# The opening of a delta-rule attention and feed-forward kernel: loads of values and queries moved, identity products added, beta's load moved forward

## The chip, the cores and the metric

The kernel runs on one core of a Trainium2 chip. A core has five engines that run their own instruction streams in order and meet at semaphores: PE (TensorE, matrix products and transposes into PSUM; its weight loads are listed as PEld), DVE (VectorE), ACT (ScalarE), POOL (GpSimd) and SP (SyncE, which here only issues DMA transfers). The metric is the time of one execution in microseconds (us). Before the change the median of three runs is 647.78 us (647.63 to 649.5). One further execution was profiled; the trace comes from that one.

## The reference

Two blocks follow each other. The first is a delta-rule recurrence over 768 positions, for 4 batches and 8 heads of 48 dimensions:

```python
k_n = k / (np.linalg.norm(k, axis=-1, keepdims=True) + 1e-06)
state = np.zeros((B, H, D, D))
for t in range(S):
    kt, vt, bt = (k_n[:, :, t], v[:, :, t], beta[:, :, t, None])
    y[:, :, t] = np.einsum('bhd,bhde->bhe', q[:, :, t], state)
    v_old = np.einsum('bhde,bhd->bhe', state, kt)
    state = state + bt[:, :, :, None] * np.einsum('bhd,bhe->bhde', kt, vt - v_old)
```

Its output, as 3072 tokens of 384 numbers, goes through a feed-forward block with a slope for negative values:

```python
h = x @ w_in                     # 384 -> 2048
g = np.maximum(h, 0.0) + alpha * np.minimum(h, 0.0)
return g @ w_out                 # 2048 -> 384
```

All of it is in 32-bit floats.

## The kernel before

The 768 positions are cut into 12 chunks of 64. A step is one chunk of two of the four batches, so there are 24 steps, numbered in order; steps 0 and 1 are the first chunk, 2 and 3 the second. Within a step the recurrence is solved in closed form: the Gram matrix of the keys is made on PE (`grams`, L486), a triangular inverse of it on DVE, and products on PE with it give the corrected values, the output and the new state. Two finished steps make 256 tokens, which go through the feed-forward block on PE (`ffn_in` L1075, `ffn_out` L1118 and faster forms later). From about 43 us on, this feed-forward work is woven between the attention pieces of later steps, so that PE always has something to do. Before that there is none, and the kernel is a chain of small pieces: this is the opening, and the change lies in it and in the function behind it.

All the order is written out by hand (the block `manual_schedule`): every engine executes its instructions in the order in which the program text makes them. What the reader needs of it:

- Loads. `load_early(n)` loads the key of step n (two transfers of 96 KB), into one of four tiles `ke0` to `ke2` and `kl1`. The first three keys are issued half on SP and half on ACT; everything else is issued by SP, one after the other. `load_v` and `load_q` load values and queries, two transfers per step. `beta_sb` (L188) is one transfer of 96 KB. `fetch_in(n)` issues the loads of the first n pieces of `w_in`, each 512 KB, into staging space; there are twelve pieces, p0 to p11 here, and `w_out` comes in sixteen pieces after them, by the same function.
- Weight conversion. Each staged piece is worked on by ACT twice (L240 and L242, `begin_in`), by DVE once (L256) and by POOL once (L263). Only then may PE use it. The feed-forward product of chunk 0 takes p0, p1, p2 for its first 12 products, p3, p4, p5 for the next 12, and so on, one piece for each third of the contraction.
- `pause(n, upto)` is a one-element write by POOL (L1668) into a staging tile that is still in use; the loads that `fetch_in(upto)` issues into that tile have to wait for it. So the point in POOL's order at which the write stands sets when the load may start.
- The opening, steps 0 to 3 together: PE makes the five `identities` (L1551) while the first loads come, then transposes of the keys (`flipped`, L430), Gram matrices (L486), transposes of beta (`betas`, L330), transposes of the queries (`query_flip`) and `queries` (L1567). ACT squares the keys (`squared`, L386), copies transposes out of PSUM and scales (`pick`, `raw`). DVE sums (`norms`, L393), picks the diagonal blocks (L643), and then runs `eliminate_small`, a triangular inverse in 28 dependent instructions. `signs` are four small instructions, alternating between DVE (L338) and ACT (L340), that take beta out of PSUM.
- While DVE eliminates, PE transposes keys 4 to 6 and queries 2 and 3 and fills the rest with products that nobody reads: `busy(n, p)` (L1539) multiplies n times 512 columns of the tile `ke2` with the identity.
- `first_chunk` then does steps 0 and 1: `place_small` (L706, DVE), `scale_first` (L845, values times norms), `matrix` and `own_values` (L857), three rounds (L857 on PE, L912 on DVE), `outputs`, `to_ffn`.
- `second_pair` does steps 2 and 3 with the feed-forward products of chunk 0 between (`alongside(products, pieces)` puts so many products of `ffn_in` and so many half steps of weight conversion there). POOL scales the values of steps 2 and 3 here (`scale_first`), and makes the turned copies `turn_matrix` and `turn_values` (L873).

Of the kernel before, what the change touches and what calls it, by code (L numbers as in the profile page):

```python
# [39 lines left out]
STAGED = 4  # L40
# [3 lines left out]
def kernel(  # L44
# [11 lines left out]
    nc = tc.nc  # L56
# [17 lines left out]
    doubles, big, ffn_banks = ExitStack(), [], []  # L74
# [49 lines left out]
    ident = const.tile([128, 128], FP32, name="ident")  # L124
# [14 lines left out]
    def load_early(n, *queues):  # L139
        if n < N:  # L140
            fetch(k, n, early(n)[:, :, 0:D], *queues)
# [15 lines left out]
    def load_q(n):  # L157
        if n < N:
            fetch(q, n, q_pad[n % NQ][:, :, 0:D])

    def load_v(n):
        if n < N:
            v_raw[n] = work.tile([128, H, D], FP32, name="v_raw", bufs=3)
            fetch(v, n, v_raw[n])
# [14 lines left out]
        mybir.EngineType.PE, mybir.EngineType.DVE, mybir.EngineType.Activation,  # L179
        mybir.EngineType.Pool, mybir.EngineType.SP,  # L180
    }))
    for i in range(2):
        load_early(i, (nc.sync, nc.scalar))

    SPACES = 3
    space_out = const.tile([128, SPACES, DM * 2], U32, name="space_out")
    beta_sb = space_out.rearrange("p s e -> p (s e)")[: B * H, 0:S].bitcast(FP32)
    nc.sync.dma_start(out=beta_sb, in_=beta.rearrange("b h s -> (b h) s"))  # L188
    load_early(2, (nc.scalar, nc.sync))

    w_in = const.tile([128, KT, DFF], FP32, name="w_in")
# [133 lines left out]
    def betas(first, last, p):  # L325
        n = last - first
        p = p[:, 0 : n * B * H].rearrange("p (c b t h) -> p c b t h", c=n, b=NB, t=2)
        for c in range(n):
            at = (first + c) * 128
            nc.tensor.transpose(  # L330
                p[:, c].rearrange("p b t h -> p (b t h)"), beta_sb[:, at : at + 128],
                ident[: B * H, : B * H],
            )
        to = beta_t.rearrange("p (c i) b h -> p i c b h", i=2)[:, :, first:last]

        def turned_sign(t, i):
            if i == 0 and first == 0:
                nc.vector.tensor_scalar_mul(to[half(t), i], p[half(i), :, :, t], -1.0)  # L338
            else:
                nc.scalar.mul(to[half(t), i], p[half(i), :, :, t], -1.0)  # L340

        return [lambda t=t, i=i: turned_sign(t, i) for t in range(2) for i in range(2)]
# [41 lines left out]
    def squared(n):  # L384
        ksq[n] = work.tile([128, H, D], FP32, name="ksq", bufs=2)
        nc.scalar.square(ksq[n], early(n)[:, :, 0:D])  # L386
# [13 lines left out]
    def weigh(n):  # L400
        if n >= N:
            return []
        norm = stats[n]
        root(norm)
        return [lambda: weigh_rest(n, norm)]
# [30 lines left out]
    def flipped(n, p):  # L436
        flip(early(n), p)
        k_t[n] = work.tile([128, G, 128], FP32, name="k_t", bufs=EARLY + 1)
        return [lambda: nc.scalar.copy(k_t[n].rearrange("p g i -> p (g i)")[0:ROWS], p[0:ROWS])]
# [26 lines left out]
    def now(pieces):  # L466
        for x in pieces:
            x()
# [368 lines left out]
    def scale_first(n, engine=nc.gpsimd):  # L837

        c, bp = steps[n]
        nv[n] = v_raw.pop(n)  # L840
        rhs_[n] = work.tile([128, 2, G, D], FP32, name="r")
        w = stats[n][0]
        x, w = (y.rearrange("p (g a) d -> p a g d", a=2) for y in (nv[n], w[:, :, None]))
        for to, own, a in ((slice(0, 128),) * 2 + (0,), (half(0), half(1), 1), (half(1), half(0), 1)):
            engine.tensor_tensor(  # L845
                out=rhs_[n][to, a], in0=x[own, a], in1=w[own, a].to_broadcast([own.stop - own.start, G, D]),
                op=ALU.mult,
            )
# [37 lines left out]
    def turn_matrix(n, engine):  # L886
        m, turned_m, _, _ = step_space(n)
        swapped(engine, turned_m, m[:, 1])
# [645 lines left out]
    def busy(n, p=None):  # L1534

        p = ps_one() if p is None else p
        while n > 0:
            x = p[:, 0 : int(512 * min(n, 1))]
            nc.tensor.matmul(  # L1539
                x, ident, k_early[2].rearrange("p h d -> p (h d)")[:, 0 : x.shape[-1]]  # L1540
            )
            n -= 1
# [3 lines left out]
        for _ in range(n):  # L1546
            nc.tensor.matmul(p[0:32, 0:32], ident[0:32, 0:32], ident[0:32, 0:32])

    def identities(n):
        for _ in range(n):  # L1550
            nc.tensor.matmul(big[1][:, 0, 0:128], ident, ident)  # L1551

    def query_flip(n, p):

        flip(q_pad[n % NQ], p)
        q_t[n] = beside[steps[n][1]][:, :, :, D : D + C]
        return lambda: nc.scalar.copy(
            q_t[n].rearrange("p t g i -> p g t i")[0:ROWS],
            p.rearrange("p (g t i) -> p g t i", g=G, t=2)[0:ROWS],
        )  # L1560
# [91 lines left out]
    n = 2 * W_IN_P  # L1652
# [9 lines left out]
    fetch_in, begin_in, conv_in = weights(pieces, stages, ids, in_done, STAGED, len(pieces))  # L1662
# [3 lines left out]
    def pause(n, upto):  # L1666

        nc.gpsimd.memset(in_stages[n][0:1, 0:1].bitcast(FP32), 0.0)  # L1668
        fetch_in(upto)
# [29 lines left out]
    def key(n):  # L1699
        return flipped(n, ffn_banks[n % 2])  # L1700
# [1 line left out]
    def gram(n):  # L1702
        return grams(n, big[n % 3 or n // 3], n // 3)

    identities(5)
    for n in (0, 2, 3):
        copy_late(n)
    squared(0)
    copy_0 = key(0)
    signs = betas(0, 1, big[2][:, 0])  # L1710
    norms(0)
    now(copy_0)
    now(signs)
    gram_0 = gram(0)
    squared(1)
    copy_1 = key(1)
    norms(1)
    pick(0, gram_0, 0)
# [37 lines left out]
    turned_q = query_flip(0, ffn_banks[1])  # L1756
    load_q(2)
    turned_q()
    turned_q = query_flip(1, ffn_banks[0])
    load_q(3)  # L1760
    fetch_in(STAGED)
# [2 lines left out]
    raw(2, gram_2)  # L1764
    raw(3, gram_3)
    nc.scalar.mul(minus, minus, -1.0)
    for n in (2, 3):
        load_v(n)
    mask = queries(big[0])
    slopes()  # L1770
    for n, p in ((5, ffn_banks[0]), (6, big[2][:, 0])):
        now(flipped(n, p))
    busy(3.6, big[1][:, 0])
    copy_4 = flipped(4, big[2][:, 1])
    now(copy_4)
    begin_in(1)
    busy(1.0, big[1][:, 0])
    for n in (2, 3):
        query_flip(n, ffn_banks[3 - n])()
    begin_in(2)  # L1780
    busy(1.3, big[1][:, 0])
    eliminate_small()

    def convert(n):
# [8 lines left out]
    def alongside(products, pieces, *gens):  # L1793
        gens = [(part(first_in, products), products), (part(convert_on, pieces), pieces), *gens]
        weave(*[x for x in gens if x[1] > 0])

    def second_pair():

        n, m, x = 2, 3, NJ
        both = (n, m)  # L1800

        def burst(step, width):
            p = ps_big()
            pieces = []
            for i in range(2):
                pieces += step(n + i, p[:, :, i * width : (i + 1) * width])
            now(pieces)

        def keys(k):
            if k == x + 3:  # L1810
                flip_more(k)
            squared(k)
            norms(k)
            load_early(k + NKE)

        def through(i, p):
            now(through_state(i, None, p))

        now(next_state(0))
        scale_first(n)  # L1820
        pause(STAGED + 2, STAGED + 5)
        scale_first(m)
        alongside(2, 2)
        now(next_state(1))
        keys(x)
        fetch_in(STAGED + 6)
        alongside(3, 3)
        burst(matrix, G * C)
        for i in both:
            turn_matrix(i, nc.gpsimd)  # L1830
        now(weigh(x))
        alongside(3, 2)
        for i in both:
            load_q(i + 2)
        fetch_in(12)
        alongside(2, 1)
        keys(x + 1)
        alongside(2, 1)
        y = ps_big()
        through(n, y[:, :, 0 : G * D])  # L1840
        alongside(2, 1)
        through(m, y[:, :, G * D : 2 * G * D])
        now(weigh(x + 1))
        alongside(2, 1)
        now(grams(x))
        alongside(2, 2)
        burst(own_values, G * D)
        pause_out(0, 2)
        for i in both:
            turn_values(i, nc.gpsimd)  # L1850
        alongside(2, 1)
        keys(x + 2)
        fetch_out(3)
        load_v(4)
        alongside(2, 2)
        now(grams(x + 1))
        alongside(2, 2)
        burst(lambda i, p: one_round(i, 0, p), G * D)
        now(weigh(x + 2))
        alongside(2, 1)  # L1860
        keys(x + 3)
        alongside(2, 1)
        now(grams(x + 2))
        alongside(2, 1)
        burst(lambda i, p: one_round(i, 1, p), G * D)
        now(weigh(x + 3))
        alongside(2, 1)
        now(grams(x + 3))
        alongside(2, 1)
        burst(lambda i, p: one_round(i, 2, p), G * D)  # L1870
        fetch_out(4)
        alongside(3, 2, (part(blocks, 2), 2))
        burst(outputs, G * D)
        alongside(4, 3)
        for i in both:
            to_ffn(i)
        squares(x + 4)
        alongside(2, 1, (part(blocks, 2), 2))
        alongside(IN_PARTS - 43, 0, (part(blocks, 2), 2))
# [21 lines left out]
    n = WHOLE + PIECES - BEGUN - SOON  # L1901
# [28 lines left out]
    n = OUT_PARTS - few - 2 * rest + 1  # L1930
# [131 lines left out]
```

## Time and profile before

| What | us |
|---|---|
| median of the three runs | 647.78 |
| the three runs | 649.5, 647.63, 647.78 |
| the profiled execution | 648.86 |
| its span, first to last instruction | 647.10 |
| PE busy in the span | 632.3 |
| PE busy from 120 us to the end (527.0 us) | 521.86 |
| granted TensorE clock, mean over the span | 0.995 |

The profiled execution took 648.86 us, of which 647.10 lie between the first and the last instruction and 1.76 outside. It is 1.08 us above the median of the runs that were not profiled. The times in the trace are counted from the start of the span. A group line of the timeline gives the start, the time from first to last, the engine, the program line, the operation with its operands, the number of instruction records, and in square brackets the idle time of the engine before it with what ended it. PE writes two records for a 32-bit product and one for a transpose.

### The profile page before, as it was taken

To read this page: it belongs to the slowest core of one execution; us is meant where nothing else is said; L and a number is where in the kernel's file an instruction comes from. 1 tells how busy PE (TensorE), PEld (TensorE's weight loads), DVE (VectorE), ACT (ScalarE), POOL (GpSimd) and SP (SyncE) were. 2 spreads that over 40 slices of the span, in tenths; PEclk is the share of its full clock that TensorE was granted. 3 is DMA by queue.
4 is the path that set the end of the run, shared out by engine and by line. 5 is a ranking of instruction groups with operands and counts; after the bars stand their busy time and mean duration, and the time that the engine had idled before them with its cause. 6 is when DMAs were issued, how large, how long until landed. Compare 5 with 4: busy or idle time off the path is not lost.

```text
span 647.1 us, 21355 instructions
## 1 busy us (share of the span) xinstructions
PE 632.3 (98%) x9159; PEld 558.9 (86%) x9159; DVE 483.2 (75%) x1157; ACT 259.4 (40%) x605; POOL 126.4 (20%) x251
## 2 busy tenths in 40 slices
PE   7889999999999999999999999999999999999997
PEld 6567787567889989989989989989999999999997
DVE  5868689978998788578678577678868568477383
ACT  6678555245553253254154144034045054042240
POOL 7188510010001000000000010000044053062360
PEclk9799999999999999999999999999999999999999
DMA  7869753113511320321210211121220210100000
GB/s 122 201 187 223 212 135 87 22 30 63 99 27 29 75 50 2 69 39 21 59 29 15 46 32 26 38 44 21 45 43 17 54 23 2 38 3 3 24 1 26
DMA packets 106799, 36.89 MB, mean 57 GB/s; under 512 B 99872, under 2 KB 103088, under 8 KB 106704
## 3 DMA queue, kind: packets, MB, share of 16 engines
q1 hardware_dynamic: 104832, 35.03, 24.4%
q8 instruction: 72, 1.18, 0.7%
q10 hardware_dynamic: 1872, 0.49, 0.4%
q14 instruction: 23, 0.19, 0.1%
HBM read 30.78 MB, written 4.72 MB: 55 GB/s over the span
## 4 chain that ended last, share of the span: by engine, by line
PE 80%; DVE 8%; DMA 4%; ACT 3%; POOL 1%; issue 1%; SPq 1%; POOLq 0%; ACTq 0%; DVEq 0%
PE p_ffn L1075 20%; PE p_ffn L1140 17%; PE p_more L1392 8%; PE p_more L1308 5%; PE p_ffn L1118 4%; PE p_ffn L1298 3%; PE p_ffn L1392 3%; PE p_ffn L1303 2%; PE p_pair L430 2%; PE p_pair L807 2%; PE p_pair L747 2%; PE p_pair L917 2%; PE p_pair L930 2%; PE p_pair L486 1%; PE p_pair L795 1%
## 5 line engine op out<-in xcount | busy, mean ns | idle before, releaser
L1075 PE MATMUL p_ffn<-xt,w_in 128*128 128x256 f32 x768 | 177.5, 384 | 1.1 <-DVE act L1087 0.5
L1075 PEld LDWEIGHTS p_ffn<-xt,w_in 128*128 128x128 f32 x768 | 142.0, 190 | 21.9 <-issue 2.0
L1087 DVE SCALAR_TENSOR_TENSOR act<-act,al_t,p_ffn 128x256 f32<-128x256 f32 x112 | 48.5, 474 | 21.1 <-ACT act L1085 21.0
L1085 ACT ACTIVATE act<-p_ffn 128x512 f32<-128x512 f32 x56 | 33.3, 595 | 77.1 <-PE p_ffn L1075 76.8
L1332 POOL TENSOR_TENSOR k_t<-k_t 128x128 f32<-128x128 f32 (+1 forms) x48 | 29.5, 615 | 167.5 <-ACT k_t L1327 165.0
L571 DVE TENSOR_TENSOR block<-block,prod 128x30 f32<-128x30 f32 (+9 forms) x150 | 50.0, 333 | 5.2
L565 DVE TENSOR_TENSOR prod<-block 128x30 f32<-128x30 f32 (+9 forms) x150 | 49.1, 327 | 4.2 <-POOL block L555 2.7
L419 POOL TENSOR_TENSOR beta_t<-beta_t,rec 128x8 f32<-128x8 f32 x20 | 5.1, 254 | 237.5 <-DVE rec L413 221.7
L1140 PE MATMUL p_ffn<-w_out,act 128*128 128x192 f32 x288 | 49.6, 328 | 0.0
L1140 PEld LDWEIGHTS p_ffn<-w_out,act 128*128 128x128 f32 x288 | 46.5, 190 | 0.3
L973 ACT COPY xt<-p_pair 128x384 f32<-128x384 f32 x22 | 10.4, 477 | 90.6 <-PE p_pair L969 76.8
L1332 POOL TENSOR_TENSOR block<-block 128x128 f32<-128x128 f32 (+1 forms) x48 | 27.7, 576 | 16.7 <-ACT block L1327 14.2
L1298 PE MATMUL p_ffn<-xt,w_in 128*128 128x256 f32 x96 | 28.7, 381 | 0.5 <-DVE o_sb L1160 0.5
L759 ACT COPY inv<-p_pair 32x256 f32<-32x256 f32 x40 | 14.5, 362 | 24.9 <-DVE u L921 24.1
L1346 DVE SCALAR_TENSOR_TENSOR act<-block,al_t,act 128x256 f32<-128x256 f32 x32 | 19.7, 657 | 5.2 <-ACT block L1342 5.1
L1160 DVE TENSOR_TENSOR o_sb<-u,p_ffn 128x192 f32<-128x192 f32 x24 | 7.9, 351 | 20.4 <-PE p_ffn L1140 20.0
L799 ACT COPY y<-p_pair 128x384 f32<-128x384 f32 x22 | 10.5, 479 | 30.4 <-PE p_pair L795 28.8
L1327 ACT COPY k_t<-p_more 128x512 f32<-128x512 f32 x16 | 9.4, 587 | 31.4 <-PE p_more L1308 26.7
L825 DVE TENSOR_TENSOR r<-v_raw,p_pair 64x192 f32<-64x192 f32 (+1 forms) x60 | 21.2, 353 | 1.0
L1392 PE MATMUL p_more<-w_out,act 128*128 128x192 f32 x128 | 21.9, 329 | 0.0
L921 DVE TENSOR_TENSOR u<-p_pair,wgt 128x384 f32<-128x384 f32 x20 | 11.1, 556 | 14.0 <-PE p_pair L747 14.0
L807 PE MATMUL p_pair<-beside,k_t 48*64 48x112 f32 x704 | 21.4, 259 | 0.2 <-ACT beside L458 0.2
(285 smaller groups left out, 1418.0 us busy)
## 6 DMA issues: line engine op xcount, KB each, us to landing
v_raw<-in_v_dram SPq DMA_DIRECT2D x48, 96.0 KB, 2.9
qp<-in_q_dram SPq DMA_DIRECT2D x48, 96.0 KB, 2.9
out_dram<-o_sb SPq DMA_DIRECT2D x90, 48.0 KB, 1.6
space_out<-in_moe_w_out_dram SPq DMA_DIRECT2D x11, 384.0 KB, 4.0
ke<-in_k_dram SPq DMA_DIRECT2D x43, 96.0 KB, 3.1
kl<-in_k_dram SPq DMA_DIRECT2D x80, 48.0 KB, 2.6
w_out<-in_moe_w_in_dram SPq DMA_DIRECT2D x6, 512.0 KB, 4.8
w_out<-in_moe_w_out_dram SPq DMA_DIRECT2D x5, 384.0 KB, 4.9
```

The costliest lines, as they stand in the source:

```text
L565: nc.vector.tensor_tensor(out=prod, in0=r[:, 0:j, j : j + 1].to_broadcast([128, j, n]), in1=r[:, j : j + 1, j + 1 : HB].to_broadcast([128, ...
L571: nc.vector.tensor_tensor(out=r[:, 0:j, j + 1 : HB], in0=r[:, 0:j, j + 1 : HB], in1=prod, op=ALU.add)
L807: nc.tensor.matmul(p[half(t ^ a), a, g], k_t[n][dims(a), g, half(t)], beside[bp][dims(a), t, g])
L1075: nc.tensor.matmul(p_h[:, i], w_in[:, t, (f + i) * 128 : (f + i + 1) * 128], xt[:, t], start=(t == 0), stop=(t == KT - 1),)
L1085: nc.scalar.activation(g, p_h, ACT.Relu, scale=-1.0)
L1087: nc.vector.scalar_tensor_tensor(out=g[:, i], in0=g[:, i], scalar=al_t[:, f + i : f + i + 1], in1=p_h[:, i], op0=ALU.mult, op1=ALU.add,)
L1118: nc.tensor.matmul(p_o[u], gs[f // 2][:, f % 2, u * 128 : (u + 1) * 128], w_out[:, f], start=(f == 0), stop=(f == FT - 1),)
L1140: nc.tensor.matmul(p, x(i), w(i), start=(i == 0), stop=(i == FP - 1))
L1298: nc.tensor.matmul(p[:, f * 256 : f * 256 + 256], w(2, f), xt[:, 2], start=True, stop=False)
L1308: nc.tensor.matmul(q[:, j], a, b, start=True, stop=True)
L1332: nc.gpsimd.tensor_tensor(out=dst, in0=a, in1=b, op=ALU.add)
L1392: nc.tensor.matmul(p, x(i), w(i), start=(i == 0), stop=(i == FP - 1))
```

## The change

The diff, whole but for its line numbers in the head of each part:

```diff
@@ load_early and beta @@
-    for i in range(2):
-        load_early(i, (nc.sync, nc.scalar))
+    load_early(0, (nc.sync, nc.scalar))
...
     nc.sync.dma_start(out=beta_sb, in_=beta.rearrange("b h s -> (b h) s"))
+    load_early(1, (nc.sync, nc.scalar))
     load_early(2, (nc.scalar, nc.sync))
@@ identities @@
-    def identities(n):
+    def identities(n, p):
         for _ in range(n):
-            nc.tensor.matmul(big[1][:, 0, 0:128], ident, ident)
+            nc.tensor.matmul(p[:, 0:128], ident, ident)
@@ opening @@
-    identities(5)
+    identities(6, big[1][:, 0])
...
     copy_0 = key(0)
+    identities(1, big[1][:, 0])
     signs = betas(0, 1, big[2][:, 0])
     norms(0)
     now(copy_0)
-    now(signs)
     gram_0 = gram(0)
     squared(1)
+    now(signs)
     copy_1 = key(1)
...
     turned_q()
+    identities(3, big[0][:, 0])
     turned_q = query_flip(1, ffn_banks[0])
...
     nc.scalar.mul(minus, minus, -1.0)
-    for n in (2, 3):
-        load_v(n)
+    identities(2, big[0][:, 0])
     mask = queries(big[0])
     slopes()
-    for n, p in ((5, ffn_banks[0]), (6, big[2][:, 0])):
+    busy(3.2, ffn_banks[0])
+    for n, p in ((6, big[2][:, 0]), (5, ffn_banks[0])):
         now(flipped(n, p))
-    busy(3.6, big[1][:, 0])
-    copy_4 = flipped(4, big[2][:, 1])
-    now(copy_4)
     begin_in(1)
-    busy(1.0, big[1][:, 0])
+    busy(1.8, big[1][:, 0])
+    now(flipped(4, big[2][:, 1]))
+    busy(0.6, big[1][:, 0])
     for n in (2, 3):
         query_flip(n, ffn_banks[3 - n])()
     begin_in(2)
-    busy(1.3, big[1][:, 0])
+    busy(1.2, big[1][:, 0])
     eliminate_small()
@@ second_pair @@
         now(next_state(0))
-        scale_first(n)
-        pause(STAGED + 2, STAGED + 5)
-        scale_first(m)
+        pause(STAGED + 2, STAGED + 3)
+        load_v(n)
+        fetch_in(STAGED + 4)
+        load_v(m)
+        fetch_in(STAGED + 5)
         alongside(2, 2)
...
         for i in both:
             turn_matrix(i, nc.gpsimd)
+            scale_first(i)
         now(weigh(x))
         alongside(3, 2)
-        for i in both:
-            load_q(i + 2)
         fetch_in(12)
...
         now(weigh(x + 3))
+        for i in both:
+            load_q(i + 2)
         alongside(2, 1)
```

In words, in the order of the program. Beta's transfer goes ahead of SP's half of key 1. There are six identity products at the start and one after the transposes of key 0. On ACT the squares of key 1 go ahead of its two signs. Three identity products stand between the two query transposes, two ahead of `queries`. The values of steps 2 and 3 are no longer loaded there. The first filler stands ahead of the transposes of keys 5 and 6, whose order is exchanged, and the fillers have 3.2, 1.8, 0.6 and 1.2 times 512 columns in place of 3.6, 1.0 and 1.3. In `second_pair` the write that lets p6 load stands ahead of the scaling; p6, the values of step 2, p7, the values of step 3 and p8 are issued in this order; each step's scaling follows its `turn_matrix` on POOL, ahead of the weights of the next key and of the conversion of p5. The queries of steps 4 and 5 are loaded later, between two pieces of `w_out`.

## The prediction

> **What bounds the kernel now.** I read the page first: busy shares, then the clock row.
>
> ```profile
> PE 632.3 (98%) x9159; PEld 558.9 (86%) x9159; DVE 483.2 (75%) x1157; ACT 259.4 (40%) x605; POOL 126.4 (20%) x251
> ...
> PEclk9799999999999999999999999999999999999999
> ```
>
> PE is the bound of the whole; the granted clock has one dip, in the second slice of 16 us. From 120 us on PE is busy for 521.86 of 527.0 us, and nothing of the change reaches there. So it is worth only what it does to PE's idle or slow time ahead of 120 us. The next view is the windows of the opening (columns: window, its length, busy time and records of PE, PEld, DVE, ACT, POOL, clock, DMA share, GB/s).
>
> ```profile
> 13.83:17.24 3.41, 2.09 (x71) 1.55 (x69) 3.17 (x9) 3.35 (x13) 3.13 (x8) 1.00 0.72 124
> 17.24:20.65 3.41, 2.24 (x22) 2.09 (x14) 3.03 (x12) 2.75 (x9) 0.41 (x1) 0.50 1.13 249
> 20.65:24.07 3.42, 3.42 (x6) 1.35 (x5) 3.02 (x12) 0.59 (x1) 0.00 (x0) 0.50 0.94 149
> 30.90:34.30 3.40, 2.20 (x136) 1.98 (x130) 2.67 (x5) 3.17 (x8) 3.28 (x5) 1.00 0.00 0
> ```
>
> The clock is halved from 17.24 to 24.07, after a stretch in which PE was busy for 2.09 of 3.41 us. A stretch with 2.20 of 3.40 (the last line) halved nothing. What that costs is in PE's timeline:
>
> ```profile
> 14.87 0.62 PE L430 MATMUL p_ffn<-ident,qp 128*112 128x128 f32 x4 [0.75 <-ACT beta_t L340]
> ...
> 16.70 0.69 PE L1567 MATMUL p_pair<-beside,k_t 48*64 48x64 f32 x32 [0.57 <-ACT beside L1557]
> ...
> 18.78 1.07 PE L430 MATMUL p_ffn<-ident,ke 128*112 128x128 f32 x4 [1.17 <-DMA ke<-in_k_dram]
> ...
> 28.77 0.69 PE L857 MATMUL p_pair<-inv,sums 64*64 64x64 f32 x32
> ```
>
> From 18.78 to 28.77 PE has no idle time, and L857 at 28.77 is the first product that needs the eliminated blocks. DVE had them earlier:
>
> ```profile
> 26.34 1.29 DVE L706 TENSOR_TENSOR inv<-inverse,block 128x512 f32<-128x512 f32 x2
> 27.55 1.10 DVE L845 TENSOR_TENSOR r<-v_raw,first_norm 128x192 f32<-128x192 f32 x3
> 30.05 0.56 DVE L895 COPY act<-p_pair 128x384 f32<-128x384 f32 x1 [1.40 <-PE p_pair L857]
> ```
>
> The first of the two L706 is done at about 27.0, and DVE then idles 1.40 us until PE's products come: here PE, slowed and full of filler, is late by 1.4 to 1.8 us.
>
> **The change, part by part; each cost against the profiled execution, 648.86 us (span 647.10 and 1.76 around it).**
>
> *Start.* Five identity products took 2.50 us (1.53 to 4.03), so one is 0.50 at that speed. The sixth ends at 4.53, 0.20 after key 0 let PE go on (4.33); the seventh lies where PE waited 0.56 for beta. Key 0's copy moves from 5.46 to 5.66. ACT's squares of key 1 stood at 7.16, behind two signs at 6.54 and 6.95; now they start when that copy ends, 6.25, if key 1 is there: its SP half is issued at about 2.25 instead of 1.59, plus the median 3.8 of these loads is 6.05. DVE's sum of them waited 0.80, to 7.72; it comes at about 7.1. PE, with no stand from 3.6 on, may also reach full speed before 10.2: a Gram matrix takes 1.13 us at 9.17 and 0.69 at 10.89. Together DVE's chain up to the elimination moves forward by 0.6: more needs POOL's weights (L622, ending at 15.0), which sit in POOL's order behind copies that end at 9.6. Bounds: 0.2 later (the sixth product alone) to 0.9 earlier.
>
> *The five identity products between.* 512 columns of filler take 0.86 us at full clock (25.82 to 26.68), so 128 take 0.22, three 0.65 and two 0.43: they fit the stands of 0.75 and 0.57. At half clock they would be 2.2 us together, ending near 18.8, and what hides them then is the wait for key 5.
>
> *That wait stays.* The 1.17 us ahead of 18.78 is key 5's transfer landing. The new filler of 3.2 stands there, but `busy` reads `ke2`, the tile that key 5 is loaded into, so it waits for the same transfer. Gain nothing. All SP issues up to key 5 keep their number, so it lands as before.
>
> *PE from 18.78.* Before: 3,020 columns of filler and five groups of four transposes at 0.44 (26.68 to 27.56 for two groups). At full clock 3,020 x 0.86 / 512 = 5.07, plus 2.20, is 7.27; the 5.29 us up to 24.07 at half clock do 2.65 of it, so 2.64 is lost: 18.78 + 7.27 + 2.64 = 28.69, and the trace has 28.77. After: 3,480 columns, 5.85 + 2.20 = 8.05, at full clock throughout 26.83. `own_values` reaches DVE 1.28 after that first product (28.77 to 30.05), at 28.11; DVE, 0.6 earlier, is free at 28.05. The rounds, `outputs` and the first feed-forward products follow in chain, so all moves forward by 30.05 - 28.11 = **1.9 us**. Bounds: 1.2 if DVE is 0.2 late; 2.7 if in addition the L256 at 31.98 takes 0.42 instead of 1.22 (it ran beside POOL's L263 from 31.62 to 32.91).
>
> [...]
>
> *POOL in the second pair.*
>
> ```profile
> 38.51 2.38 POOL L845 TENSOR_TENSOR r<-v_raw,first_norm 128x192 f32<-128x192 f32 x3
> ...
> 41.01 1.84 POOL L845 TENSOR_TENSOR r<-v_raw,first_norm 128x192 f32<-128x192 f32 x3
> ...
> 48.84 1.30 POOL L263 TENSOR_TENSOR w_in<-w_out,w_in 128x512 uint32<-128x512 uint32 x1
> ```
>
> The two L845 leave the place ahead of p3 and p4 and go between the turned copies, ahead of p5 (48.84). In the clock of before, so without the 1.9: p6 may be loaded at 38.6 instead of 41.07, which takes away ACT's wait of 2.0 us for it at 45.10, so the matrix copies follow PE's products (end 44.96) at 45.06, and POOL turns at 45.6. Then 0.83 + 1.65 + 0.84 + 1.65 (the turned copies took 0.83 and 0.84 at 46.38 and 47.25, an undisturbed L845 group took 1.65 at 15.99) + 0.7 for the weights puts p5's conversion at 51.4 to 52.8. PE's 15th feed-forward product, the first that needs p5, started at 51.94: a new stand of 0.9. Behind it PE had a stand of 0.51 at 68.90 for DVE, which takes up about that much: **+0.45** (bounds 0 and 1.2). The value loads (four issues, 0.7 each) leave SP at 23.31, where nothing queued until 35.64, and stand between p6, p7 and p8; these were needed at 45.1, 48.0 and 49.8 and leave at 38.7, 40.5 and 42.3. Nobody waits longer.
>
> *The queries of steps 4 and 5.* Four issues (4.71 us at 44.76) leave the queue ahead of p10 and p11; p10's reader waited 0.2, so no gain on the path. They now stand behind the first of four `w_out` loads (65.62). ACT already waits there:
>
> ```profile
> 74.64 0.57 ACT L240 ACTIVATE w_out<-w_out 128x384 uint32<-128x384 uint32 x1 [1.49 <-DMA w_out<-in_moe_w_out_dram]
> ...
> 76.86 0.58 ACT L1085 ACTIVATE act<-p_ffn 128x512 f32<-128x512 f32 x1
> ```
>
> Four issues at 0.65 are 2.6 us, of which SP had 0.8 to 1.3 to spare on the next load (1.46 where 0.43 is the median). So the piece for 74.64 comes about 1.3 later, ACT's L1085 with it, and behind that the freeing of the bank that PE needs, where 0.5 was to spare (DVE's L1087 end 78.35, PE's next product 78.87): **+0.8** (bounds 0 and 1.6, the whole 2.1 less the 0.5).
>
> Sum: 648.86 - 1.9 + 0.45 + 0.8 = 648.2. Against the median, which lies 1.08 below the profiled execution, 647.78 - 0.65 = **647.1**.
>
> **Rivals.** *The gain carries.* The stand for p5 and the later `w_out` piece are covered, as the stand at 68.90 covers a part, and the L256 runs free: -1.9 - 0.65, median 645.2. For it: every load that moves away left a queue earlier, and DMA carried 22 and 8 GB/s at 57 and 58 us. Against: POOL's order is fixed, and 0.9 is counted from rows.
>
> *The clock falls again.* PE now fills its stands early, so it is ahead and waits longer for key 5: from about 17.3 (the last small transposes) to 18.78 it is idle, which leaves about 1.95 of the 3.41 us to 20.65, less than the 2.09 that halved the clock. If the rule is PE's busy share, 20.65 to 24.07 runs at half: 1.7 lost, 28.5, gain 0.25. If it is halved from 17.24 as before, the longer filler costs 26.83 + 2.64 = 29.47, 0.70 later than 28.77. Then +0.70 + 0.45 + 0.8 is 649.7, and with the upper bounds of the last two 651.3. Against: those 1.95 us are full 128-row products, while the stretch that fell held transposes and 64-column pieces. It decides as soon as PE reaches L857 after 28.77.
>
> *It doesn't do what it says:* the stand at 18.78 is not filled, as shown; the rest of the claim holds in the instruction order.
>
> **Numbers.** No change is within 0.3%, 1.9 us, about what a measurement of this kernel can tell. The forecast, given back in part, 0.40 (0.36 within, 0.04 faster); the gain carries, 0.32 (0.31 faster, 0.01 within); the clock falls, 0.28 (0.25 slower, 0.03 within). Faster 0.35, same 0.40, slower 0.25. The range reaches to both rivals, 644.9 to 650.2; the forecast's own is 645.9 to 648.6.
>
> **What would show it.** Full clock from 17 to 28 us and L857 (the first) at about 26.8; DVE's L895 at 28.1; PE idle ahead of 18.78 still ended by a key's DMA; a PE stand of about 0.9 at the third product after 49 us less the gain, released by POOL's L263; a longer wait of ACT's L240 near 73 us. Wrong if the clock is halved again inside 20 to 27 us, if L845 between the turned copies holds nobody up, or if the first L857 is early and the products behind 40 us are not.

## The result, and the profile after

| Kernel | median, us | runs | range |
|---|---|---|---|
| before | 647.78 | 7 | 647.02 to 649.5 |
| changed | 651.18 | 7 | 650.57 to 652.8 |

The ratio of changed to before is 1.0054, with a 95% interval of 1.0038 to 1.0069: the change makes the kernel 3.5 us slower (0.0054 x 648). The forecast was 647.1, within 644.9 to 650.2. The profiled execution of the changed kernel took 650.63, with a span of 648.59; 2.04 lie outside the span, where it was 1.76 before.

Two lines of the page come first: the granted clock, and the DMA queue that the page calls "instruction" (packets, MB, share).

```profile
PEclk9999999999999999999999999999999999999999
...
q8 instruction: 72, 1.18, 0.7%
```

The dip of the second slice is gone. The windows (columns as before) show what is left of it:

```profile
13.60:17.00 3.40, 3.17 (x44) 2.69 (x47) 2.68 (x7) 2.53 (x9) 3.08 (x7) 0.56 0.80 146
17.00:20.65 3.65, 3.65 (x58) 2.12 (x47) 3.24 (x13) 2.04 (x8) 0.00 (x0) 1.00 1.15 225
```

In windows of half a microsecond the clock is halved from about 13.2 to 16.6: one stretch of 3.4 us, ahead of the fillers, instead of 6.83 us in them. The timelines of PE and DVE:

```profile
17.75 3.04 PE L1539 MATMUL p_ffn<-ke,ident 128*128 128x512 f32 x8
...
26.36 0.69 PE L857 MATMUL p_pair<-inv,sums 64*64 64x64 f32 x32 [0.26 <-DVE inv L706]
...
30.61 0.79 PE L857 MATMUL p_pair<-act 64*64 64x48 f32 x39 [0.57 <-issue]
...
40.35 0.55 PE L946 MATMUL p_pair<-u,kl 64*64 64x48 f32 x18 [1.23 <-issue]
...
51.52 1.13 PE L1075 MATMUL p_ffn<-xt,w_in 128*128 128x256 f32 x4 [1.01 <-POOL w_in L263]
...
74.68 1.01 PE L969 MATMUL p_pair<-ident,y 128*128 128x128 f32 x6 [0.96 <-DVE y L936]
...
80.05 0.67 PE L1075 MATMUL p_ffn<-xt,w_in 128*128 128x256 f32 x2 [1.34 <-ACT w_out L240]
```

```profile
25.61 1.29 DVE L706 TENSOR_TENSOR inv<-inverse,block 128x512 f32<-128x512 f32 x2
...
27.95 0.56 DVE L895 COPY act<-p_pair 128x384 f32<-128x384 f32 x1
```

The opening did what the forecast said and more: DVE's L706 starts 0.73 earlier (0.6 forecast), the first L857 comes at 26.36 (26.83 forecast, 28.77 before) and DVE's L895 at 27.95 (28.1 forecast, 30.05 before). PE is at full speed earlier in this profile, too: the Gram matrix at 8.13 takes 0.69, where the one at 9.17 took 1.13 before. PE now waits 0.26 for DVE there. But new stands follow. Two of those shown have no releaser ("issue"), the third waits for POOL, the fourth and fifth come from pieces of `w_out`. What they do to the lead is seen when starts of the same PE groups are compared (us from the start of each span; e1 and e11 are experiments below):

| PE group | before | changed | lead | e1_q_back | e11_both |
|---|---|---|---|---|---|
| first L857 | 28.77 | 26.36 | -2.41 | -2.23 | -2.31 |
| first L946 | 39.55 | 36.98 | -2.57 | -2.60 | -2.75 |
| `matrix` of the second pair, L857 | 43.80 | 42.32 | -1.48 | -1.51 | -1.39 |
| first L486 behind 50 us | 53.00 | 52.59 | -0.41 | -0.41 | -1.14 |
| `own_values` of the second pair, L857 | 54.69 | 54.43 | -0.26 | -0.42 | +0.38 |
| L930 of the second pair | 71.78 | 70.64 | -1.14 | -0.59 | -0.10 |
| L969 of the second pair | 74.87 | 74.68 | -0.19 | -0.57 | +0.21 |
| L946 behind 80 us | 81.43 | 82.82 | +1.39 | -0.57 | +0.22 |
| L486 near 93 us | 93.16 | 94.71 | +1.55 | -0.70 | +0.07 |

So 1.1 is lost between 37 and 43 us, 1.1 more ahead of 53 us, and 2.5 between 71 and 82 us; between 54 and 71 us 0.9 is won back. Behind 94 us nothing changes. POOL's and SP's part of it:

```profile
47.93 1.73 POOL L845 TENSOR_TENSOR r<-v_raw,first_norm 128x192 f32<-128x192 f32 x3
...
50.18 1.29 POOL L263 TENSOR_TENSOR w_in<-w_out,w_in 128x512 uint32<-128x512 uint32 x1
```

```profile
66.82 2.64 SPq L137 DMA_DIRECT2D qp<-in_q_dram  x4
69.90 2.26 SPq L223 DMA_DIRECT2D w_out<-in_moe_w_out_dram  x3
```

```profile
70.81 0.58 ACT L240 ACTIVATE w_out<-w_out 128x384 uint32<-128x384 uint32 x1 [3.76 <-DMA w_out<-in_moe_w_out_dram]
...
75.18 0.55 ACT L240 ACTIVATE w_out<-w_out 128x384 uint32<-128x384 uint32 x1 [2.72 <-DMA w_out<-in_moe_w_out_dram]
```

p5's conversion starts at 50.18, behind the second scaling, and PE stands 1.01 for it. In the kernel before, the same two instructions of ACT stood here:

```profile
69.89 0.55 ACT L240 ACTIVATE w_out<-w_out 128x384 uint32<-128x384 uint32 x1 [1.62 <-DMA w_out<-in_moe_w_out_dram]
...
71.95 0.59 ACT L240 ACTIVATE w_out<-w_out 128x384 uint32<-128x384 uint32 x1 [0.21 <-DMA w_out<-in_moe_w_out_dram]
```

The second piece is issued directly behind the queries (69.90) and comes 3.23 us later than before; that is PE's stand of 1.34. The first piece is issued ahead of the queries (66.17, and 65.62 before). It comes 0.92 later, and the rest of its longer wait is ACT's own lead: ACT is free at 67.04 instead of 68.27. It delays L1085 and, on DVE, L1087 and then L936, for which PE stands 0.96. That the queries cause this first wait is not shown: over the profiles with all transfers it is 2.5 to 3.8 in the seven with the queries in this place, and 1.4 to 3.7 in the seven with them elsewhere. The second wait tells the two groups apart: 1.58 to 3.04 against at most 0.59.

### The profile page after: what moved, and what is told of

Its sections match the earlier page's. It is cut to its first block, busy times and chain, and to the rows that moved or that the text cites. A ratio compares the mean times of both kernels' runs of the same rounds, so it can differ in the third digit from the quotient of the medians.

```text
span 648.6 us, 21391 instructions
## 1 busy us (share of the span) xinstructions
PE 632.7 (98%) x9177; PEld 560.3 (86%) x9177; DVE 480.6 (74%) x1157; ACT 258.5 (40%) x605; POOL 125.6 (19%) x251
## 3 DMA queue, kind: packets, MB, share of 16 engines
q8 instruction: 72, 1.18, 0.7%
## 4 chain that ended last, share of the span: by engine, by line
PE 81%; DVE 9%; DMA 3%; ACT 2%; POOL 2%; issue 2%; SPq 1%; POOLq 0%; DVEq 0%; ACTq 0%
PE p_ffn L1075 21%; PE p_ffn L1140 17%; PE p_more L1392 8%; PE p_more L1308 5%; PE p_ffn L1118 4%; PE p_ffn L1298 3%; PE p_ffn L1392 3%; PE p_ffn L1303 2%; PE p_pair L807 2%; PE p_pair L747 2%; PE p_pair L430 2%; PE p_pair L930 2%; PE p_pair L917 2%; PE p_pair L486 1%; PE p_pair L946 1%
## 5 line engine op out<-in xcount | busy, mean ns | idle before, releaser
L1087 DVE SCALAR_TENSOR_TENSOR act<-act,al_t,p_ffn 128x256 f32<-128x256 f32 x112 | 48.6, 474 | 22.3 <-ACT act L1085 22.2
L1085 ACT ACTIVATE act<-p_ffn 128x512 f32<-128x512 f32 x56 | 33.2, 594 | 77.3 <-PE p_ffn L1075 77.0
L954 DVE TENSOR_TENSOR beside<-beside,p_pair 48x384 f32<-48x384 f32 (+1 forms) x38 | 20.8, 548 | 2.5 <-PE p_pair L946 2.3
```

Of the source, the lines that this page charges most:

```text
L1085: nc.scalar.activation(g, p_h, ACT.Relu, scale=-1.0)
L1087: nc.vector.scalar_tensor_tensor(out=g[:, i], in0=g[:, i], scalar=al_t[:, f + i : f + i + 1], in1=p_h[:, i], op0=ALU.mult, op1=ALU.add,)
```

## The experiments

Theory: the opening gains, and the edits of the second pair give it back. Rivals: A, the loss is made in the opening; B, it comes from the value loads and the scaling. All ratios are to the kernel before on the same chip.

### Parts alone and parts undone

**e1_q_back**, the queries back at their former place:

```diff
         alongside(3, 2)
+        for i in both:
+            load_q(i + 2)
         fetch_in(12)
...
-        for i in both:
-            load_q(i + 2)
```

> The changed kernel with the query loads of steps 4 and 5 back at their former place. Theory (the opening gains about 2.4 us, and the query loads ahead of w_out's pieces give back 2.3 to 2.7 of it): 651.2 - 2.4 = 648.8, the wait of ACT's L240 near 75 us short, and the PE stand of 1.34 near 80 us gone. Rival A (the loss is in the opening: identities and fillers): stays at 651. Rival B (the loss comes from the value loads and POOL's scaling in the second pair): 650.5 or more.

Measured: 649.22, ratio 1.0010 (0.9996 to 1.0025). ACT's timeline:

```profile
69.67 0.56 ACT L240 ACTIVATE w_out<-w_out 128x384 uint32<-128x384 uint32 x1 [1.98 <-DMA w_out<-in_moe_w_out_dram]
...
71.54 0.58 ACT L240 ACTIVATE w_out<-w_out 128x384 uint32<-128x384 uint32 x1 [0.22 <-DMA w_out<-in_moe_w_out_dram]
```

The first wait is shorter and the second gone, and with them PE's stands at 74.68 and 80.05. Against the changed kernel's 1.0054 the queries are worth 0.0044, or 2.9 us. Rivals A and B, as whole explanations, fall.

**e2_open_only**, the opening's edits alone:

```diff
-        pause(STAGED + 2, STAGED + 3)
-        load_v(n)
-        fetch_in(STAGED + 4)
-        load_v(m)
-        fetch_in(STAGED + 5)
+        scale_first(n)
+        pause(STAGED + 2, STAGED + 5)
+        scale_first(m)
...
             turn_matrix(i, nc.gpsimd)
-            scale_first(i)
```

with `load_v(2)` and `load_v(3)` in the opening again and the queries as in e1.

> Only the edits of the opening (beta, identities, fillers, order of keys 5 and 6); the second pair as before, value loads of steps 2 and 3 in the opening again. Theory: 647.8 - 2.4, of which up to 1.2 may be lost to new stands of PE between 30 and 45 us: 645.4 to 646.6. Rival A (the loss is in the opening): 650 to 651. Rival B: as the theory.

Measured: 649.52, 1.0017 (1.0002 to 1.0031). The gain isn't there, so the theory is wrong in this half, and so is A, whose price is too high. In the profile the first L857 comes at 26.79, 1.98 ahead of before. Then PE stands 1.27 with no releaser, the granted clock is halved for 6.83 us from 32 us on, and at 39.65 (the first L946) the lead is gone.

```profile
32.44 2.29 PE L857 MATMUL p_pair<-act 64*64 64x48 f32 x71 [1.27 <-issue]
```

This execution took 651.26, which is 1.7 above the median of e2. So it shows a way in which the lead can go, not where the median lost it.

**e3_pair_only** and **e4_q_only**: the second pair's edits in the kernel before, and the queries' move alone.

```diff
         alongside(3, 2)
-        for i in both:
-            load_q(i + 2)
         fetch_in(12)
...
         now(weigh(x + 3))
+        for i in both:
+            load_q(i + 2)
```

> The kernel before with only the second pair's edits (values loaded and scaled there, queries later). Theory: the give-back alone, 2.3 to 2.7 for the queries and 0.4 to 0.9 for POOL's order, so 650.5 to 651.4. Rival A: 647.8 to 648.2, since the opening is as before. Rival B: 651 or more.

> The kernel before with only the query loads of steps 4 and 5 moved. Theory: 647.8 + 1.5 to 2.7 = 649.3 to 650.5, with ACT's L240 waiting over 2 us for a piece of w_out near 75 us. Rivals A and B, and my forecast (0.8 at most behind a spare of 0.5): 647.8 to 648.6.

Measured: e3 651.02, 1.0036 (1.0023 to 1.0050); e4 650.23, 1.0026 (1.0011 to 1.0040). Both times agree with the theory: the queries alone cost 1.7 us, and ACT's two L240 wait 2.83 and 1.89 in e4's trace (over 2 was expected near 75 us, where 1.89 stands).

**e8_scale_only**, POOL's scaling moved in the kernel before:

```diff
-        scale_first(n)
         pause(STAGED + 2, STAGED + 5)
-        scale_first(m)
...
             turn_matrix(i, nc.gpsimd)
+            scale_first(i)
```

> The kernel before with only POOL's scaling moved between the turned copies; values loaded in the opening, queries at their former place. Theory: PE stands 0.7 to 1.0 for POOL's L263 near 52 us, 0.5 of it covered at 69 us: 648.65 + 0.2 to 0.6. If the 0.28 that the value edits add outside the span belongs to this half, the time outside is 2.05 and the sum 649.1 to 649.5; if it belongs to the loads, 1.78.

Measured: 649.51, 1.0014 (0.9999 to 1.0030), and 2.04 outside the span. So the 0.28 outside come with this edit here. The expected stand for L263 near 52 us isn't in this trace: a stand of 0.84 without releaser at 49.31 came first. The singles add up: 0.0017 + 0.0026 + 0.0014 is 0.0057, against 0.0054.

**e7_p5_first**, e1 with the scaling behind p5's conversion:

```diff
             turn_matrix(i, nc.gpsimd)
-            scale_first(i)
         now(weigh(x))
         alongside(3, 2)
+        for i in both:
+            scale_first(i)
```

> The changed kernel with the query loads back at their former place and POOL's scaling behind p5's conversion instead of between the turned copies. Theory (POOL's order made PE's stand of 1.01 near 51.5 us): the stand is gone, and as that stand alone stood between e1_q_back's -1.48 and its -0.41 behind it, all after it comes up to 1.0 earlier than in e1_q_back unless DVE is waited for at 68 us: 648.2 to 649.0 against 649.2. Rival (the time was lost elsewhere and the stand is only the place where it shows): 649.2 again.

Measured: 649.73, 1.0007 (0.9994 to 1.0021). The stand for L263 is gone from PE's timeline, and 1.76 lie outside the span, but the time doesn't tell it from e1 and lies above the 648.2 to 649.0 of the theory. In its profile PE stood 0.84 and 0.99 without releaser at 30.80 and 34.80 and the clock was halved for 6.8 us from 36 us on: the next question.

### The stands without a releaser

**e5_shift** moves every later PE instruction in the program:

```diff
-    busy(1.2, big[1][:, 0])
+    short(24, big[1][:, 0])
+    busy(0.6, big[1][:, 0])
```

> The changed kernel with 24 products of 32 columns in place of 1.0 ms-free filler columns: the last filler, 512 + 102 columns, becomes 24 short products and one of 307 columns, so that every later PE instruction stands 46 matmul records further back in the stream. Theory (PE's stands with no releaser come each 128 matmul records, that is 256 instructions with the weight loads, where the next block of its program has not arrived): the stands move 46 records earlier in the program, from 14 records inside the second L946 group to 4 records after the start of the first L946 group near 37 us, and from 25 records inside the second L857 group on act to 11 records inside the first. Rival (the stands belong to what PE does there, a wait that the profile does not show): they stay at 25 and 14 records. Time between 650 and 652.5.

("1.0 ms-free" is a slip: the last filler's 614 columns are meant.) Measured: 651.61, 1.0037 (1.0022 to 1.0052). PE's timeline (the groups are cut at the stands):

```profile
30.24 1.02 PE L857 MATMUL p_pair<-act 64*64 64x48 f32 x53 [0.31 <-issue]
...
34.16 1.02 PE L857 MATMUL p_pair<-r,act 64*64 64x48 f32 x53 [0.86 <-issue]
```

A stand ahead of 53 of 64 records lies 11 records inside the first of two groups of 32, as forecast; in the changed kernel it lay ahead of 39 (7 + 32), 25 records inside the second: 46 records later. The next stand comes 128 records on. The third place that was forecast, 4 records inside the first L946 group, shows no stand: the clock was halved from 35.5 us on, and PE reached it only at 38.91. In the 14 profiles with more than one such stand, they lie a multiple of 128 records apart, within two records. With a weight load for each record, 128 records are 256 instructions. The instruction queue's line above gives 1.18 MB in 72 packets, 16.4 KB each, and PE's 9,177 products with as many weight loads make 71.7 times 256, so a packet may be 256 instructions of PE. From this I read the stands as PE waiting for the next block of its program. The traces show the distance and these sizes, not the wait itself. Between 30 and 57 us not every multiple of 128 has a stand; from 57.3 to 130 us no profile has one.

**e12_no_ident** takes away the five identity products between (ten records fewer):

```diff
-    identities(3, big[0][:, 0])
...
-    identities(2, big[0][:, 0])
```

> The changed kernel without the five identity products between the query transposes and ahead of the queries' products. If they keep the clock up: a half-clock stretch of 6.8 us between 14 and 24 us, as in the kernel before, and the first L857 at 27.5 or later. If they do not matter: at most 3.4 us at half clock, and the first L857 at 26.2 to 26.8. Time 650.5 to 652.5 either way, because the queries set when PE goes on near 80 us.

Measured: 652.75, 1.0062 (1.0041 to 1.0082). In its profile the granted clock is halved for 10.2 us between 13 and 24 us, and the first L857 comes at 29.30. With the identity products the clock stays up longer here: the eleven profiles that have them show at most 3.4 us of half clock ahead of 24 us, and four of the five with the old opening 6.8 (the fifth, e3, is spoken of at the end). The stands are ten records further on, as the block theory wants, so this one lies 24 records inside L946 instead of 14:

```profile
43.38 0.33 PE L946 MATMUL p_pair<-u,kl 64*64 64x48 f32 x8 [1.20 <-issue]
```

**e6_v_early**, the values loaded in the opening, all else as changed:

```diff
+    for n in (2, 3):
+        load_v(n)
     identities(2, big[0][:, 0])
...
         pause(STAGED + 2, STAGED + 3)
-        load_v(n)
-        fetch_in(STAGED + 4)
-        load_v(m)
         fetch_in(STAGED + 5)
```

> The changed kernel with the values of steps 2 and 3 loaded in the opening again, scaling where the change has it. Theory A (the value loads between the w_in pieces hold PE's program block back and lengthen the stand of 1.23 near 40 us): stand under 0.7, time 650.2 to 650.7, and the time outside the span 1.78 again instead of 2.05. Theory B (the loads of values are without effect): 651.2, stand as before, 2.05.

Measured: 652.0, 1.0049 (1.0028 to 1.0070), 2.04 outside the span. The stand near 42 us shrank to 0.41, as theory A said, but neither its time nor its 1.78 outside the span followed. Another stand grew:

```profile
32.95 0.79 PE L857 MATMUL p_pair<-act 64*64 64x48 f32 x39 [2.21 <-issue]
```

From 28 to 30 us the DMA share is 1.16 here, and 0.04 in the changed kernel, where this stand is 0.57. The two profiles with the changed opening, the values in it and all transfers, e2 and e6, have 1.27 and 2.21 at this place; six with later values (changed, e1, e7, e9, e10, e11) have 0.84 or less. So moving the values did shorten this stand, by a way that the forecast didn't know; the time doesn't show it (1.0049 against 1.0054).

### All three prices taken away

**e9_again** is the changed kernel once more; **e10_q_end** puts the queries behind five pieces of `w_out`; **e11_both** does this and e7's edit together.

```diff
         now(weigh(x + 3))
-        for i in both:
-            load_q(i + 2)
...
         alongside(IN_PARTS - 43, 0, (part(blocks, 2), 2))
+        for i in both:
+            load_q(i + 2)
```

> The changed kernel itself, beside the kernels before and the experiments on one chip: 651.2 and a ratio of 1.004 to 1.007, if the 1.0054 of the first comparison holds. If the ratio is 1.003 or less, the first comparison overstated the loss, and the parts measured singly (1.0026 for the queries alone, 1.0017 for the opening, 1.0014 for the scaling) are to be compared with that.

> The changed kernel with the query loads of steps 4 and 5 behind the first five pieces of w_out instead of behind the first. Theory (their place in the queue, ahead of the pieces for which ACT waits at 71 and 75 us, makes PE unable to go on before about 79.4 to 80): the two L240 wait under 2.1 together, PE's stand of 1.34 is gone, 648.8 to 649.8. Rival (any later loading of the queries costs it, through the time when they land): 651 or more. Rival (the loss is made before 70 us): 651.

> The same place for the queries, and POOL's scaling behind p5's conversion: all three prices that were found are taken away, only the opening and the later values stay. Theory that the gain of the opening (2.0 to 2.4 at the first L857) is otherwise carried: 646.3 to 647.3 against 648.7, faster. Theory that it is lost again to PE's stands for its program blocks and to the clock that falls behind them at 30 to 41 us: 648.5 to 649.7, not faster.

Measured: e9 652.31, 1.0054 (1.0032 to 1.0075), the first comparison again. e10 650.0, 1.0020 (1.0005 to 1.0035), just above the 649.8 expected. e11 649.57, 1.0022 (1.0009 to 1.0034): not faster. In e9's profile the stand for `w_out` is longer than in the changed kernel's,

```profile
81.48 0.70 PE L1075 MATMUL p_ffn<-xt,w_in 128*128 128x256 f32 x2 [1.94 <-ACT w_out L240]
```

and behind it the granted clock is halved for 3.4 us from 82 us on. In e10 the second wait is gone, the first isn't (ACT's timeline), and the 2.1 expected for both together was too low. The first can't be put down to the queries, which are issued behind both pieces here; e2 and e7, with the queries at their former place, have 3.66 and 3.01:

```profile
72.74 0.56 ACT L240 ACTIVATE w_out<-w_out 128x384 uint32<-128x384 uint32 x1 [2.81 <-DMA w_out<-in_moe_w_out_dram]
...
74.28 0.55 ACT L240 ACTIVATE w_out<-w_out 128x384 uint32<-128x384 uint32 x1
```

e11's PE timeline shows where a lead of 2.31 goes when hardly anything but stands without a releaser is in its way:

```profile
30.43 0.79 PE L857 MATMUL p_pair<-act 64*64 64x48 f32 x39 [0.28 <-issue]
...
33.88 0.33 PE L857 MATMUL p_pair<-r,act 64*64 64x48 f32 x7 [0.44 <-issue]
...
40.45 0.55 PE L946 MATMUL p_pair<-u,kl 64*64 64x48 f32 x18 [1.51 <-issue]
...
53.62 0.46 PE L486 MATMUL p_pair<-k_t 48*64 48x64 f32 x15 [1.27 <-issue]
```

The sum is 3.5 us. In the table above the lead is still 2.75 behind the first two, which replace waits for DVE, and falls by 1.36 and 1.52 at the last two. This execution took 648.93 and ends level with the one of before (+0.07 near 93 us). So it shows the lead going, and not the 1.4 us by which the medians differ (0.0022 x 648).

### Fewer transfers

**e13_light_before** and **e14_light_open** (e11 with the same edit) load 16 of 128 rows of p4 to p9; **e15_light_open2** does it with e2. These kernels leave out seven eighths of those weights and work with zeros there, so they show only times.

```diff
-                nc.sync.dma_start(out=words(i)[0], in_=pieces[i][1].bitcast(U32))
+                rows = 16 if count == 12 and 4 <= i < 10 else 128
+                nc.sync.dma_start(out=words(i)[0][:rows], in_=pieces[i][1][:rows].bitcast(U32))
...
     slopes()
+    for i in range(4, 10):
+        nc.gpsimd.memset(in_stages[i].bitcast(FP32), 0.0)
```

> The kernel before with 16 of 128 rows of w_in's pieces p4 to p9 loaded (the rest of these staging tiles is filled with zeros by POOL near 18 us, when it is idle). It leaves out 7/8 of those transfers and is the counterpart of the next run. Theory (PE's stands between 35 and 60 us are late program blocks, late because the DMA engines are full of w_in): stands with no releaser at 37 and 42 us shrink from 0.47 and 0.38 towards 0.2; time 646.5 to 648.2. Rival (the blocks take their time whatever is loaded): 647.8 to 648.8.

> e11_both (opening and later values kept; queries behind w_out; p5 first) with the same seven eighths of p4 to p9 left out. Theory: the stands of 1.51 inside the second L946 group and 1.27 inside L486 fall below 0.5 each, the opening's 2.0 to 2.4 is carried to the end, and the kernel is 1.3 to 2.4 faster than e13_light_before (e11_both was 1.5 slower than the kernel before). Rival (the stands do not depend on the loads, or the gain is lost elsewhere): within 0.7 of e13_light_before, or slower.

> e2_open_only (the opening's edits alone; second pair, values and queries as before) with the same seven eighths of p4 to p9 left out as in e13_light_before. In e14_light_open the stands near 40 and 53 us were gone or short, but PE fell back between 64 and 79 us behind POOL, whose scaling had moved into its busy time. Theory (with quiet DMA engines and POOL as before, what the opening gains is carried): first L857 at 26.3 to 27.0, no stand over 0.6 behind 35 us, ratio 0.995 to 0.9965 against 0.9978 of e13_light_before. Rival (the value loads in the opening hold the block back that PE needs near 30 us, as in e2_open_only with 1.27 and e6_v_early with 2.21, and that alone takes the gain): a stand of 1 to 2 us 25 records inside the second L857 group on act, ratio 0.997 to 0.999.

Measured: e13 646.96, 0.9978 (0.9967 to 0.9988); e14 647.31, 0.9980 (0.9965 to 0.9994); e15 647.67, 0.9984 (0.9972 to 0.9996). In e14's PE timeline (this source has one line more) the second L946 group runs through, where e11 had a stand of 1.51, and the stand of 1.27 has become 0.47:

```profile
39.19 0.68 PE L947 MATMUL p_pair<-u,kl 64*64 64x48 f32 x32
...
51.45 0.46 PE L487 MATMUL p_pair<-k_t 48*64 48x64 f32 x15 [0.47 <-issue]
```

So w_in's transfers make the first of these two stands and most of the second: that part of the theory is shown, for these two. In e13 the stand at 42 is gone as well, but the one at 37, which was to shrink from 0.47 towards 0.2, is 0.57 (ending at 36.20). Against e11 the kernel is 2.7 us faster (0.0042 x 648), of which the same edit gives 1.4 to the kernel before (e13). Its other part is not: e14 is no faster than e13. Two things stand in the way. e13's first L857 came at 27.17 without any edit of the opening, so e14 had a lead of 0.26 there and 0.88 at 46 us, not 2.3. And from 64 to 79 us e14 lost 1.3 again: POOL, which scales from 46.95 to 50.41 there, lets `w_out`'s first transfers go at 56.06 (55.34 in e13), and ACT waited 2.02 for them. e15 was to settle it. Its ratio lies outside the 0.995 to 0.9965 of its theory and inside the rival's range, but the rival's stand is not there (0.55 at 32.70), and in its profiled execution the clock was halved from 19.6 to 23.0 and the first L857 came at 28.57. So the gain isn't there, and the trace doesn't tell why.

## Why the prediction was wrong

**The opening, -1.9.** The mechanism is in the trace (-2.41 at L857), but the step that failed is the next one: that the rounds, `outputs` and the first products "follow in chain, so all moves forward". It is the prediction's own last sign of being wrong: the first L857 early, and the products behind 40 us not. Measured alone (e2) the opening is worth +1.1 us (0.0017 x 648). Two things were missed. First, PE stands without a releaser, at distances that are multiples of 128 records or 256 instructions. With the DMA engines quiet (a share of 0.02 to 0.03) the next stand ends 3.45 us after the one before in three profiles (30.61 to 34.06 in the changed kernel, 30.43 to 33.88 in e11, 31.24 to 34.69 in e10) and 3.92 in e5, and with w_in's transfers under way it takes 6.3 to 6.6 (34.06 to 40.35, 33.88 to 40.45):

```profile
34.00:40.40 6.40, 4.63 (x131) 3.49 (x131) 3.68 (x7) 4.21 (x8) 3.24 (x4) 1.00 0.87 264
```

If, as I read it, PE waits there for a block of its program, a PE that is early gets there before its block. The kernel before showed such stands as two idle times, 128 records apart, for which I had no term:

```profile
37.38 1.02 PE L930 MATMUL p_pair<-u,a_t 64*64 64x48 f32 x54 [0.47 <-issue]
...
42.31 1.56 PE L1075 MATMUL p_ffn<-xt,w_in 128*128 128x256 f32 x6 [0.38 <-issue]
```

Second, half clock often follows such a stand. Of the nine profiles with the changed opening, its identity products and all transfers, six have a half-clock stretch of 3.4 to 6.8 us that begins between 32 and 42 us; of the four with the old opening (before, e3, e4, e8) none has one behind 24 us, though e8 had a stand of 0.96 at 32.58. In those six the half clock moved from the fillers into the work. It isn't needed for the loss: in the changed kernel, e1 and e11 the clock stayed full there, and their leads shrank all the same. These two things show how a lead of 2 us comes to nothing. Why the medians lie 1.1 to 1.4 above the kernel before stays open.

**How large the lead is** was also taken too high, from one profile of the kernel before. With the old opening the first L857 came at 28.77, 28.21, 28.76, 27.14 and 27.17 (before, e3, e4, e8, e13), 28.0 on average; in the ten profiles with the new one (all others but e5 and e12, which change its products) between 26.28 and 28.57, 26.8 on average. That is 1.2, not 2.4, and just the lower bound of the forecast's 1.9 (1.2 to 2.7).

**POOL, +0.45.** The stand was forecast as 0.9 and is 1.01 in the changed kernel and 1.00 in e9. That 0.51 of it would be taken up at 68.90 came true as well: that stand is gone. e8 prices the edit at 0.9 us with an interval that reaches from 0 to 1.9, of which 0.28 lie outside the span, where I had no term.

**The queries, +0.8.** This is the term that was mis-sized: 1.7 us alone (e4), 2.9 as the difference of the changed kernel and e1. I counted the piece for 74.64, the third of the four, and it came about as late as forecast: 76.22, 1.58 later (1.3 forecast). What holds it back is the second piece, for 71.95: it stands directly behind the queries, had waited only 0.21, and comes 3.23 later. The spare behind it was smaller, too: PE's next product stood at 78.74, not 78.87, which leaves 0.39 and not 0.5. And I added the terms: a transfer sets a time before which PE can't go on, so what PE is early by is added to its wait, not taken off the end. From L969 to the product that waits for `w_out` it took 3.87 us before (74.87 to 78.74), the same in the six other profiles in which the queries stand elsewhere, and 4.3 to 6.0 in the seven with them ahead of that piece. The 0.96 that PE stood for L936 was in no term, and its cause is open.

**The range** doesn't follow from the bounds either: its top, 650.2, lies 1.1 below the 651.3 that the clock rival gave with the upper bounds, and the measured 651.18 lies between the two.

**"That wait stays."** Wrong in the changed kernel's profile: key 5 was there when the filler began at 17.75, without a stand. It holds in others: 1.36 in e2, 1.06 in e5, 0.99 in e6, each ended by a key's DMA.

**The clock rival** gave 649.7 for a fall between 17 and 24 us. There it didn't happen, and in the changed kernel's own profile nowhere behind 16.6; in six others it happened at 32 to 42 us. The length of a stand alone doesn't tell whether the clock falls: ahead of e9's fall at 82 us PE stood 1.94 us, ahead of e7's at 36 us 0.99, and behind the 1.23 of the changed kernel and the 1.51 of e11 it didn't fall.

No experiment with all its transfers beats the kernel before. What stays open: whether the opening's gain would be carried without these stands, what puts the 0.28 outside the span, and when exactly the clock falls.

## What to carry to other kernels

Terms of a sum add only along one chain: where a transfer, or as read here a block of the program, sets a time before which nothing goes on, work made early turns into waiting, so ask of every gain which fixed time comes next. An idle time that the profile can't put down to anything is a term too: see whether such stands lie at equal distances in the instruction count, and price them for a stream that runs faster. Small loads put between two large ones that an engine waits for delayed the one behind by about their own time in the queue here (2.64 us of issues, and the piece came 2.5 to 3.2 later in e4 and the changed kernel); the piece after it came 1.58 later in the changed kernel.

## What the runs showed of the hardware

- PE stands with no releaser, of 0.2 to 2.2 us, at multiples of 128 matmul records (256 instructions) between 30 and 57 us. From the end of one such stand to the end of the next: 3.45 to 3.92 us with a DMA share of 0.02 to 0.03 (changed, e5, e10, e11, e14, e15), 3.42 to 4.00 with 0.14 to 0.20 (e7, e8, e12), 4.93 with 0.60 (before), 6.3 with 0.87 (changed) and 6.6 with 0.90 (e10, e11), but 5.74 with 1.01 (e12).
- Six profiles have a half-clock stretch that began between 0.2 us ahead of and 1.7 us behind the end of a stand of 0.86 to 2.21 us, all between 32 and 42 us; behind the 1.23 of the changed kernel and of e1, the 1.51 of e11 and the 0.96 of e8, the clock stayed full.
- In e3's profile the granted clock reads full throughout, while 64 records of L1567 took 1.99 us instead of 1.20 in the changed kernel, about as at half clock (eight of L1539 took 4.61 instead of 3.04), and a Gram matrix at 9.28 took 1.13, as at the start of the others. By these times the column missed a stretch there, the whole opening up to about 23 us.
- 2.04 to 2.08 us outside the span with the scaling between the turned copies, 1.76 to 1.79 without, over nine and five kernels with all transfers. But e13, e14 and e15, which have the scaling elsewhere and POOL fill six tiles with zeros, have 2.00 to 2.04, so the 0.28 isn't tied to this edit alone.
